# Spreading loads, decay products and routing steps through the attention loop of a three-stage kernel

## The chip, the cores and the metric

One core of one Trainium2 chip runs the whole program. The metric is the device time of one execution in microseconds (us), as the median of several executions. Three executions of the kernel before are given, and one more was profiled.

## The reference

Three layers follow each other, all in fp32, on 3072 tokens (4 batches of 768) of 256 features (8 heads of 32).

```python
def reference(x, a, B, C, ...):
    attn = _attn_ref(x, a, B, C)             # decaying linear attention, per batch and head
    t = attn.transpose(0, 2, 1, 3).reshape(3072, 256)
    t = _moe_ref(t, w_gate, w1, w2)          # 8 experts, each token goes to the best one
    return _moe2_ref(t, probs, v1, v2)       # 4 experts, all of them, mixed by probs

# attention: state (16 x 32) per head;  y_i = C_i . state_i,
#   state_i = a_i * state_(i-1) + outer(B_i, x_i)
# moe:  e = argmax(t @ w_gate);  out = softmax(t @ w_gate)[e] * relu(t @ w1[e]) @ w2[e]
# moe2: out = sum over 4 experts of p_e * relu(t @ v1[e]) @ v2[e]
```

## The kernel before

The program has three stages, one behind the other on TensorE. Stage 1, the attention with the routing of its tokens, takes about the first 105 us of the trace; stage 2, the 8 experts, goes on to about 278 us; stage 3, the 4 dense experts, fills the rest.

**Stage 1** cuts the 3072 tokens into 24 units of 128 (`NU = 24`, six units to a batch, `NCH = 6`), each made of two chunks of 64. The order of its instructions on every engine is the order of the code (`tc.manual_schedule`), and the loop at L728, `for i in range(NU + 2)`, is a software pipeline: iteration i does the last steps of unit i and the first ones of units i+1 and i+2. For a unit u the steps are

- `decay` (L459): TensorE spreads the decays a into `abc`, and a VectorE scan (L465) turns them into `Lt`, the products of decays inside a chunk;
- `decayed_b` (L475): GpSimd multiplies B into `br`, in two halves, one instruction for each chunk;
- `decayed_c` (L549): GpSimd multiplies C, in the padded form `cz`, with the running products `pf` into `Cs`;
- `scores` (L488, L490): TensorE multiplies B and the heads of C (`cm`) into `cb`, and VectorE multiplies with `Lt` into `M`;
- `gain` (L536) and `state` (L544): TensorE sums B x into `U`, and a VectorE scan carries the state `S`, one per chunk;
- `within`, `across`, `copy_y` (L502, L514, L520): TensorE makes `y` from `M` and from `S`, and ScalarE copies it to `yT`;
- `stage_c`, `store` (L560, L568, L569, L570): TensorE transposes `yT` and multiplies it with the gate weights into `tp`, ScalarE takes the logits `lg` and the tokens `xo` out of it, and SyncE's queue stores `xo` to `xs` in DRAM.

The running products `pf` (and `pfg`, the same at the chunk ends) come for three units at a time from `decays_c` (L444, L446, L448): one product `pfp` of TensorE with the selection matrix `sel`. Its other operand is made by `chunk_products` (L388 to L396) once for each half of a batch's length, in tiles named `spare`: a scan in fp32 (L393), its rounding to fp32r by ScalarE (L395), and the rest that the rounding left by GpSimd (L396), so that 64 rows, high parts and rests, enter an fp32r product. The first half is made ahead of the loop, the second in the iterations 0 and 1, and `decays_c(1)` stands in iteration 2 in front of `scores`. All products of this kind share two PSUM buffers named `abc` with `abc` itself and with the counts of the routing.

**Loads** all stand in SyncE's queue: B and x by unit pairs (`load`, L432, L433, 128 and 256 KB), and for three units at once B and C in the transposed form (`load_bc`, L329 to L334: `CT`, `BT`, and C a second time into the two planes of `cz`). The weights of expert 0 come in pieces (`WEIGHTS`, L138); the first weights are split into a high and a low part inside the loop (`split_w`: L154 ScalarE, L160 GpSimd), the second weights behind it (L918 to L920; L154 ScalarE, L158 VectorE). `idd<-zero` (L748) writes 128 words of 4 bytes to DRAM in iteration 8.

**Routing** (`route`) takes the logits of a group of units, finds the expert and the place of each token, and adds the tokens' numbers to the lists `idxf` by small products (`invert`; `om` L226, `ip` L238). `ENDS` names the last units of the groups: 13, 7 and 4 units here, and one more that is empty. The steps of a group are appended to the list `queue`, and `slot` takes one or two of them off at fixed places of each iteration. Behind the first group (`EARLY = 12`) `early` gathers the first 256 tokens of expert 0 from `xs` (`gather`, L280, two indirect DMAs in one step), and eight empty steps later `make_x` transposes them, so that their first product (`ahead`, `pha`) can be made in iteration 24. What is left in `queue` runs behind the loop.

**Stage 2** starts with the 256 early tokens of expert 0 and then needs `idx` (L613), the end of the last group, for the gathers of all others. TensorE does two matmul groups per expert (`ph` L263, `po` L906). **Stage 3** is one dense run of TensorE (L1203, L1264).

These lines set the group ends and the places of the loop's work:

```python
EARLY = 12
ENDS = (12, 19, 23)
    WEIGHTS = {5: (0, 0), 9: (0, 1), 13: (1, 0), 17: (1, 1)}
    SPLITS = {9: 0, 13: 1}
    if i == 2:
        decays_c(1)
    if i % 3 == 1 and has(i + 2) and i > 1:
        decays_c((i + 2) // 3)
    if i == NU:
        ahead(0)
```

Of the kernel before, what the change touches and what calls it, by code (L numbers as in the profile page):

```python
# [8 lines left out]
F32 = mybir.dt.float32  # L9
# [10 lines left out]
P = 128  # L20
# [3 lines left out]
L = 64  # L24
# [9 lines left out]
EARLY = 12  # L34
ENDS = (12, 19, 23)
# [7 lines left out]
def body(tc, I, out):  # L43
    nc = tc.nc
    with ExitStack() as outer:
# [79 lines left out]
        wsp = [outer.enter_context(tc.tile_pool(name="w1s", bufs=1))]  # L125

        def load_w(g, which, j, queue=nc.sync, pieces=1):
# [9 lines left out]
            n = shp[0] // pieces  # L137
            fs = [lambda a=a: queue.dma_start(raw[:, a:a + n], src[:, a:a + n]) for a in range(0, shp[0], n)]  # L138
# [4 lines left out]
        def split_w(g, which, j, parts=1):  # L143
# [158 lines left out]
        with ExitStack() as ctx:  # L302
# [16 lines left out]
            def load_bc(i, cuts=(), queue=nc.sync):  # L319
# [3 lines left out]
                CT = lp.tile([P, HB], F32, tag="CT", name="CT", bufs=3)  # L323
# [4 lines left out]
                def part(a, e, queue=nc.sync):  # L328
                    queue.dma_start(CT[:, a:e], I["CT"][b][:, s0 + a:s0 + e])  # L329
                    queue.dma_start(BT[:, a:e], I["BT"][b][:, s0 + a:s0 + e])  # L330

                def padded(a, e):
                    for m in range(2):
                        nc.sync.dma_start(cz[i % NBC][m::2, m, a:e], I["CT"][b][m::2, s0 + a:s0 + e])  # L334

                def head(h, a, e):
                    nc.scalar.activation(cm[:, h, a:e], CT[:, a:e], AF.Copy, scale=hmask[:, h:h + 1])

                if cuts:
                    return part, padded, head  # L340
                part(0, HB)
                padded(0, HB)
                return [lambda h=h: head(h, 0, HB) for h in range(4)]

            bc_part, bc_padded, bc_head = load_bc(0, (P,))
            bc_part(0, P, nc.scalar)
            d0 = ac.tile([P, 1], F32, name="d0")
# [4 lines left out]
            def spare(tag, dt=F32):  # L352
                return m1.tile([P, 2, 512], dt, tag=tag, name="spare").rearrange("p k c -> p (k c)")[:L, :S]

            a2, d1, pr, prh = spare("xh"), spare("xl").rearrange("p (k i) -> p k i", i=L), spare("xh"), spare("xl", F32R)
            nc.sync.dma_start(a2, I["a2"])
            cz = [ac.tile([P, 2, HB], F32, name=f"cz{k}") for k in range(NBC)]
            NBR = 3
            BW = 2 * P + 2
            brs = [ac.tile([P, 2, BW], F32, name=f"br{k}") for k in range(NBR)]  # L360
            pfg = [ac.tile([P, 3, HD, 3], F32, name=f"pfg{k}") for k in range(3)]
            selF = ac.tile([P, L], F32, name="selF")
            nc.vector.tensor_add(selF, ident[:, :L], ident[:, L:])
            hm8 = ac.tile([P, 4, 2], F32, name="hm8")
            nc.vector.tensor_reduce(hm8, ident.rearrange("p (q n m) -> p q m n", q=4, m=2), axis=AX.X, op=ALU.add)
            hmask = ac.tile([P, 4], F32, name="hmask")
            nc.vector.tensor_add(hmask.rearrange("p (q m) -> p q m", m=2), hm8[:, :2], hm8[:, 2:])
            sel32 = ac.tile([L, L // 2], F32, name="sel32")
            nc.vector.tensor_add(sel32, selF[:L, :L // 2], selF[:L, L // 2:])
            pick = ac.tile([P, 2 * NU, L], F32R, name="pick")  # L370
            delta = ac.tile([P, H, L], F32, name="delta")
            sel = ac.tile([L, NB, P], F32R, name="sel")

            def select(a, e):
                nc.scalar.copy(pick[:, a:e], selF[:, a:e, None].broadcast_to([P, e - a, L]))

            def select_heads(b):
                o = sel[:, b].rearrange("c (q n a) -> c q n a", q=4, a=2)
                nc.scalar.copy(o, sel32[:, b * H:b * H + H].rearrange("c (q a) -> c q a", a=2)[:, :, None, :]
                               .broadcast_to([L, 4, DS, 2]))  # L380

            def chunk_products(h):
# [19 lines left out]
            nc.vector.memset(cz[0], 0.0)  # L402
            select(0, 8)
# [22 lines left out]
            def load(b):  # L426
                bt = lp.tile([P, NCH, P], F32, tag="bt", name="bt")
                x = lp.tile([P, NCH, D], F32, tag="x", name="x")
                x_, b_ = (I[k][b].rearrange("p (c d) -> p c d", c=NCH) for k in ("xt", "bt"))

                def part(a, e):
                    nc.sync.dma_start(bt[:, a:e], b_[:, a:e])  # L432
                    nc.sync.dma_start(x[:, a:e], x_[:, a:e])  # L433

                st[b] = dict(x=x, bt=bt)
                return part
# [3 lines left out]
            def decays_c(i):  # L440
# [3 lines left out]
                nc.tensor.matmul(ps, sel[:, b], prh[:, h * HB:h * HB + HB], start=True, stop=True)  # L444
                PF[i] = lp.tile([P, 3, P], F32, tag="pf", name="pf", bufs=3)
                nc.scalar.copy(PF[i].rearrange("p c i -> p (c i)"), ps)  # L446
                ends = ps.rearrange("p (c k i) -> p c k i", c=3, k=2)[..., L - 1:L].rearrange("p c k o -> p c (k o)")
                nc.scalar.copy(pfg[i % 3][..., 1:], ends[:, :, None, :].broadcast_to([P, 3, HD, 2]))  # L448
# [10 lines left out]
            def decay(u):  # L459

                abc = pa.tile([P, H, L], F32, tag="abc", name="abc", bufs=2)
                nc.tensor.matmul(abc, pick[:, 2 * u:2 * u + 2].rearrange("p c j -> p (c j)"),
# [909 lines left out]
```

## Time and profile before

| what | value |
|---|---|
| three executions | 812.77, 813.72, 806.47 us |
| their median | 812.77 us |
| profiled execution | 806.2 us |
| its span (first to last instruction) | 804.5 us |
| mean granted clock of TensorE | 0.98 |
| PE, DVE, ACT, POOL busy | 95%, 71%, 51%, 59% of the span |

PE is TensorE, DVE VectorE, ACT ScalarE, POOL GpSimd, SP SyncE; SPq rows are the issuing of DMAs from its queue. The span is 1.7 us shorter than the profiled execution's time. The three executions lie at two levels, and the profiled one lies at the lower. TensorE's clock has two levels, 1.2 and 2.4 GHz; a granted clock of 1.00 is the higher one all through a stretch, 0.50 the lower one.

### The profile page before, as it was taken

To read this page: it belongs to the slowest core of one execution; us is meant where nothing else is said; L and a number is where in the kernel's file an instruction comes from. 1 tells how busy PE (TensorE), PEld (TensorE's weight loads), DVE (VectorE), ACT (ScalarE), POOL (GpSimd) and SP (SyncE) were. 2 spreads that over 40 slices of the span, in tenths; PEclk is the share of its full clock that TensorE was granted. 3 is DMA by queue.
4 is the path that set the end of the run, shared out by engine and by line. 5 is a ranking of instruction groups with operands and counts; after the bars stand their busy time and mean duration, and the time that the engine had idled before them with its cause. 6 is when DMAs were issued, how large, how long until landed. Compare 5 with 4: busy or idle time off the path is not lost.

```text
span 804.5 us, 17552 instructions
## 1 busy us (share of the span) xinstructions
PE 767.7 (95%) x6891; PEld 722.8 (90%) x6891; DVE 567.5 (71%) x983; ACT 411.4 (51%) x903; POOL 472.0 (59%) x533
## 2 busy tenths in 40 slices
PE   7989878999999999999999999999999999999994
PEld 5555568889999889999999999999999999999994
DVE  7646763784456678678796777887777977778853
ACT  4755343444455465546655455556455555554540
POOL 6546625835776065448866366786355877475634
PEclk9989988999999999999999999999999999999997
DMA  6584324546533300000101000000000100000001
GB/s 191 155 177 142 95 31 157 191 124 96 156 119 95 91 27 27 2 1 27 32 23 27 1 1 27 28 27 27 1 1 1 53 2 2 1 34 21 27 27 53
DMA packets 42117, 46.62 MB, mean 58 GB/s; under 512 B 10928, under 2 KB 30512, under 8 KB 42032
## 3 DMA queue, kind: packets, MB, share of 16 engines
q1 hardware_dynamic: 37328, 37.16, 17.2%
q0 software_dynamic: 3360, 7.13, 2.9%
q10 hardware_dynamic: 1344, 1.18, 0.5%
q8 instruction: 55, 0.90, 0.5%
q14 instruction: 30, 0.25, 0.1%
HBM read 39.10 MB, written 6.35 MB: 56 GB/s over the span
## 4 chain that ended last, share of the span: by engine, by line
PE 62%; ACT 1%; DVE 1%; issue 0%; POOL 0%; POOLq 0%; DVEq 0%; ACTq 0%
PE po L1264 33%; PE x L1203 9%; PE z L1203 8%; PE w L1203 8%; PE y L1203 4%; PE poA L1264 0%; ACT s L1216 0%; ACT xc L849 0%; POOLq L1368 0%; ACT h L1209 0%; DVE h L1212 0%; DVE ts L840 0%; DVE c L1230 0%; DVE c L1238 0%; POOL out L1284 0%
## 5 line engine op out<-in xcount | busy, mean ns | idle before, releaser
L1264 PE MATMUL po<-w,h 128*128 128x256 f32 x2280 | 280.0, 280 | 0.3 <-DVE h L1212 0.3
L1264 PEld LDWEIGHTS po<-w,h 128*128 128x128 f32 x2280 | 277.5, 188 | 0.5 <-DVE h L1212 0.5
L1209 ACT ACTIVATE h<-c 128x384 fp32r<-128x384 f32 x192 | 98.8, 525 | 150.2 <-DVE c L1238 85.0
L1212 DVE SCALAR_TENSOR_TENSOR h<-c,h 128x384 fp32r<-128x384 f32 x192 | 149.6, 788 | 11.5
L1221 POOL TENSOR_TENSOR g<-s,s 128x384 f32<-128x384 f32 x64 | 65.1, 1017 | 150.5 <-ACT s L1220 148.7
L1223 DVE TENSOR_TENSOR u<-y,s 128x384 f32<-128x384 f32 x64 | 35.5, 555 | 70.0 <-ACT s L1220 65.1
L1203 PE MATMUL x<-xc,wh 128*128 128x384 f32 x256 | 67.0, 342 | 3.6 <-ACT s L1216 1.5
L1203 PE MATMUL w<-xc,wh 128*128 128x384 f32 x256 | 66.0, 338 | 0.5 <-ACT xc L849 0.4
L1203 PE MATMUL z<-xc,wh 128*128 128x384 f32 x256 | 65.4, 337 | 0.0
L160 POOL TENSOR_TENSOR wl<-raw,wh 128x1024 fp32r<-128x1024 f32 (+1 forms) x22 | 39.6, 1801 | 40.7 <-ACT wh L154 29.0
L850 POOL TENSOR_TENSOR xc<-x,xc 128x384 fp32r<-128x384 f32 x32 | 36.9, 1153 | 44.5 <-ACT xc L849 44.2
L885 ACT ACTIVATE hh<-ph 128x216 fp32r<-128x216 f32 (+8 forms) x68 | 33.5, 494 | 51.2 <-PE ph L263 43.4
L1238 DVE TENSOR_TENSOR c<-u,g 128x384 f32<-128x384 f32 x64 | 59.3, 927 | 0.0
L1216 ACT COPY s<-x 128x384 f32<-128x384 f32 x64 | 30.6, 478 | 52.3 <-PE x L1203 51.9
L887 DVE SCALAR_TENSOR_TENSOR hl<-ph,hh 128x216 fp32r<-128x216 f32 (+8 forms) x68 | 37.6, 558 | 24.3 <-ACT hh L885 24.2
L1212 DVE SCALAR_TENSOR_TENSOR h<-x,h 128x384 fp32r<-128x384 f32 x64 | 35.7, 558 | 24.5 <-ACT h L1209 24.2
L850 POOL TENSOR_TENSOR xc<-ts,xc 128x384 fp32r<-128x384 f32 x46 | 52.3, 1149 | 0.0
L263 PE MATMUL ph<-xh,wh 128*128 128x488 f32 (+8 forms) x142 | 49.4, 351 | 1.1 <-ACT xo L569 0.6
L263 PE MATMUL ph<-xl,wh 128*128 128x488 f32 (+8 forms) x142 | 49.5, 348 | 0.0
L263 PE MATMUL ph<-xh,wl 128*128 128x488 f32 (+8 forms) x142 | 49.2, 347 | 0.0
L1203 PEld LDWEIGHTS x<-xc,wh 128*128 128x128 f32 x256 | 42.2, 188 | 7.7 <-ACT s L1216 5.3
L906 PE MATMUL po<-hh,wh 128*128 128x488 f32 (+8 forms) x142 | 48.8, 343 | 0.0
(245 smaller groups left out, 1704.9 us busy)
## 6 DMA issues: line engine op xcount, KB each, us to landing
raw<-in_w SPq DMA_DIRECT2D x26, 512.0 KB, 4.0
raw<-in_v SPq DMA_DIRECT2D x32, 256.0 KB, 2.7
x<-in_xt SPq DMA_DIRECT2D x12, 256.0 KB, 3.3
xs<-xo SPq DMA_DIRECT2D x24, 128.0 KB, 2.5
bt<-in_bt SPq DMA_DIRECT2D x12, 128.0 KB, 2.3
CT<-in_CT SPq DMA_DIRECT2D x7, 192.0 KB, 3.0
BT<-in_BT SPq DMA_DIRECT2D x7, 192.0 KB, 2.9
cz<-in_CT SPq DMA_DIRECT2D x14, 96.0 KB, 4.0
```

Of the source, the lines that this page charges most:

```text
L160: ins = nc.gpsimd.tensor_sub(lo[:, :, a:a + n], raw[:, :, a:a + n], hi[:, :, a:a + n].bitcast(F32))
L263: mm = nc.tensor.matmul(ph, w[:, k, fs], x[k], start=(i == 0), stop=(i == 5))
L850: eng.tensor_sub(o[:, 1], src, o[:, 0].bitcast(F32))
L887: i1 = nc.vector.scalar_tensor_tensor(hl, ph, 0.0, hh.bitcast(F32), op0=ALU.max, op1=ALU.subtract)
L906: mm = nc.tensor.matmul(po, w[:, f % 4, ks], h, start=(i == 0), stop=(i == 23))
L1203: nc.tensor.matmul(bank[to], w[:, a], x[:, r], start=(m == 0 and to not in seen), stop=(m == 2), skip_group_check=True)
L1209: sc.activation(HP[n][0], src, AF.Relu)
L1212: v.scalar_tensor_tensor(HP[n][1], src, 0.0, HP[n][0].bitcast(F32), op0=ALU.max, op1=ALU.subtract)
L1221: nc.gpsimd.tensor_add(g_, s5, s7)
L1223: v.tensor_add(u2, bank["y"], s1)
L1238: v.tensor_add(c22, u2, g_)
L1264: nc.tensor.matmul(two[h], x[:, ts], w2[:, w, j], start=(i, j, h * (len(hs) - 1), m) == (0, 0, 0, 0), stop=(i, j, m) == (3, 1, 2), skip_gr ...
```

## The change

What it does, part by part:

- **Loads.** B and x come by single units, four units ahead (64 and 128 KB). `CT` is gone: the heads of C are made from `cz`. Of `BT` and the two planes of `cz` one is issued per iteration. The weights of expert 0 come as sixteen pieces of 128 KB, one per iteration from iteration 3 to 18; of the first weights a piece is now a quarter of the columns.
- **Decays.** `chunk_products` ends with the scan; `pfp` is one fp32 product of 32 rows. L395 and L396 are gone. The seven `decays_c` of the loop stand in the iterations 2, 3, 4, 5, 6, 9 and 12, behind `decay`; ahead of the loop the order of the first units is changed. `pick` (eleven casts ahead) becomes `pk`, one small cast per unit.
- **Routing.** The groups are 12, 7 and 5 units. The counting of `early` moves into the first group's steps, and `ie`, the two gathers and `make_x` are taken one per iteration. `ahead(0)` is called behind the loop.
- **Expert 0's second weights** are split inside the loop, in eight pieces, ScalarE the high and GpSimd the low parts.

The diff, cut to its core:

```diff
-EARLY = 12
-ENDS = (12, 19, 23)
+EARLY = 11
+ENDS = (11, 18, 23)
...
+            n, c = shp[0], shp[1] // pieces
+            if which:
+                n, c = shp[0] // pieces, shp[1]
...
-                if which:
+                if which and parts == 1:
                     nc.vector.tensor_sub(lo[:, :, a:a + n], raw[:, :, a:a + n], hi[:, :, a:a + n].bitcast(F32))
                     return
...
-                CT = lp.tile([P, HB], F32, tag="CT", name="CT", bufs=3)
...
-                    nc.scalar.activation(cm[:, h, a:e], CT[:, a:e], AF.Copy, scale=hmask[:, h:h + 1])
+                    nc.scalar.activation(cm[:, h, a:e], cz[i % NBC][:, h % 2, a:e], AF.Copy, scale=hmask[:, h // 2:h // 2 + 1])
...
                 def products():
                     nc.vector.tensor_tensor_scan(pr[:, s], a2[:, s], d1[:, k].rearrange("p k i -> p (k i)"), 0.0,
                                                  op0=ALU.mult, op1=ALU.add)
-                    nc.scalar.copy(prh[:, s], pr[:, s])
-                    nc.gpsimd.tensor_sub(prh[L // 2:, s], pr[L // 2:, s], prh[L // 2:, s].bitcast(F32))
...
+            def load(u):
+                b, c = divmod(u, NCH)
...
+                nc.sync.dma_start(st[b]["bt"][:, c], I["bt"][b].rearrange("p (c d) -> p c d", c=NCH)[:, c])
+                nc.sync.dma_start(st[b]["x"][:, c], I["xt"][b].rearrange("p (c d) -> p c d", c=NCH)[:, c])
...
-                nc.tensor.matmul(ps, sel[:, b], prh[:, h * HB:h * HB + HB], start=True, stop=True)
+                nc.tensor.matmul(ps, sel[:, b], pr[:, h * HB:h * HB + HB], start=True, stop=True)
...
-                ] + invert(rt, sl, g0, n, NC, finish, psum, rest=2 if last else 5)
+                ] + list(between) + invert(rt, sl, g0, n, NC, finish, psum, rest=2 if last else 3)
...
+                return ([count, None, shift],
+                        [lambda: nc.vector.tensor_scalar(ie, idxf[:, 0:2], float((EARLY + 1) * P - 1), None, op0=ALU.min)]
+                        + [lambda k=k: gather(0, (k,), xs[:(EARLY + 1) * P], ie) for k in range(2)] + [None]
+                        + [lambda: make_x(0, (0, 1), psum_a)])
...
+            for h in range(4):
+                bc_head(h, P, HB)
+            warm(2)
             decay(1)
-            warm(4)
             decays_c(0)
...
+            WEIGHTS = {3: (0, 0), 7: (0, 1), 11: (1, 0), 15: (1, 1)}
+            SPLITS = {8: (0, 0), 12: (0, 1), 16: (1, 0), 20: (1, 1)}
+            DECAYS = {max(m + 1, 3 * m - 9): m for m in range(1, NU // 3)}
...
+                if has(i + 4):
+                    load(i + 4)
...
                 if has(i + 2):
                     decay(i + 2)
+                if i < 2:
+                    chunks[2 + i]()
+                if i in DECAYS:
+                    decays_c(DECAYS[i])
+                if has(i + 1):
+                    decayed_c(i + 1)
+                for f in gathers[:1]:
+                    if f:
+                        f()
+                gathers = gathers[1:]
                 slot(2)
...
-                if i == NU:
-                    ahead(0)
...
+                    between, after = early() if i - 2 == EARLY else ((), ())
+                    queue += route(*GROUPS[i - 2], psum_a, between)
+                    if after:
+                        queue.append(lambda after=after: gathers.extend(after))
+            assert not gathers
+            ahead(0)
             queue += route(*GROUPS[NU - 1], psum_p)
...
-            for j in range(2):
-                for f in split_w(0, 1, j):
-                    f()
```

Three places of the order on the engines follow. On TensorE, at the end of iteration 1 and in iteration 2 (`pfp` is the product of the running decays for the units 3 to 5, `cb` the scores of unit 3), before:

```order
L514 MATMUL y<-Cs,S 32x128 x8
L536 MATMUL U<-x,br_145 32x32 x16
L560 MATMUL tp<-rhsT_179,yT 128x136
L560 MATMUL tp<-rhsT_180,yT 128x136
L444 MATMUL pfp<-spare,sel 128x384
L488 MATMUL cb<-cm,BT 64x256 x4
L462 MATMUL abc<-ah,pick 128x512
```

and now:

```order
L507 MATMUL y<-Cs,S 32x128 x8
L529 MATMUL U<-x,br_146 32x32 x16
L553 MATMUL tp<-rhsT_184,yT 128x136
L553 MATMUL tp<-rhsT_185,yT 128x136
L481 MATMUL cb<-cm,BT 64x256 x4
L455 MATMUL abc<-ah,pk 128x512
L437 MATMUL pfp<-spare,sel 128x384
```

`pfp` has moved behind the scores and the `abc` of the same iteration.

On GpSimd, about the two gathers of expert 0's early tokens (`wl` is a low part of its weights, `ex` a routing step), before:

```order
L475 TENSOR_TENSOR br_145<-bt,Lt 64x2x64 x2
L549 TENSOR_TENSOR Cs<-cz_140,pf 128x256
L475 TENSOR_TENSOR br_143<-bt,Lt 64x2x64 x2
L549 TENSOR_TENSOR Cs<-cz_141,pf 128x256
L280 DMA xg<-xs,ie 128x256 x2
L475 TENSOR_TENSOR br_144<-bt,Lt 64x2x64 x2
L549 TENSOR_TENSOR Cs<-cz_141,pf 128x256
```

and now:

```order
L163 TENSOR_TENSOR wl_0_1_1978<-raw_0_1_1537,wh_0_1_1977 128x4x64
L468 TENSOR_TENSOR br_146<-bt,Lt 64x2x64 x2
L542 TENSOR_TENSOR Cs<-cz_130,pf 128x256
L283 DMA xg<-xs,ie 128x256
L610 TENSOR_TENSOR ex<-lg,mx 128x56
L163 TENSOR_TENSOR wl_0_1_1978<-raw_0_1_1537,wh_0_1_1977 128x4x64
L468 TENSOR_TENSOR br_147<-bt,Lt 64x2x64 x2
L542 TENSOR_TENSOR Cs<-cz_130,pf 128x256
L283 DMA xg<-xs,ie 128x256
```

The two gathers stand in two units, and every unit there has a `wl` as well.

On VectorE, at the start of the second group's routing (`mx` is its first step; 128x7 is the group of seven units, 128x4 the last of four), before:

```order
L490 TENSOR_TENSOR M<-cb,Lt 128x512
L544 SCALAR_TENSOR_TENSOR S<-pfg_147,U 128x96
L158 TENSOR_TENSOR wl_0_0_2329<-raw_0_0_1317,wh_0_0_2328 128x1024
L297 TENSOR_TENSOR xl<-tpx,xh 128x2x256
L623 TENSOR_REDUCE mx<-lg 128x7
L624 TENSOR_TENSOR eq<-lg,mx 128x56
L158 TENSOR_TENSOR wl_0_1_2333<-raw_0_1_1675,wh_0_1_2332 128x1024
L625 TENSOR_TENSOR eq<-eq,rev 128x56
L623 TENSOR_REDUCE mx<-lg 128x4
```

and now:

```order
L537 SCALAR_TENSOR_TENSOR S<-pfg_151,U 128x96
L616 TENSOR_REDUCE mx<-lg 128x7
L483 TENSOR_TENSOR M<-cb,Lt 128x512
L617 TENSOR_TENSOR eq<-lg,mx 128x56
L458 SCALAR_TENSOR_TENSOR Lt<-abc,delta 128x512
L618 TENSOR_TENSOR eq<-eq,rev 128x56
L619 TENSOR_REDUCE m_2051<-eq 128x7
L620 TENSOR_TENSOR oneh<-eq,m_2051 128x56
L621 TENSOR_REDUCE red<-oneh 128x8
L537 SCALAR_TENSOR_TENSOR S<-pfg_151,U 128x96
```

The second group's first steps have moved from behind the last unit to between the units 21 to 23; the two `wl` of VectorE are gone.

## Rows read from the trace of the kernel before

**Rows 1.** The page: the span, and the chain that ended last by line.

```profile
span 804.5 us, 17552 instructions
...
PE po L1264 33%; PE x L1203 9%; PE z L1203 8%; PE w L1203 8%; PE y L1203 4%; PE poA L1264 0%; ACT s L1216 0%; ACT xc L849 0%; POOLq L1368 0%; ACT h L1209 0%; DVE h L1212 0%; DVE ts L840 0%; DVE c L1230 0%; DVE c L1238 0%; POOL out L1284 0%
```

**Rows 2.** Timeline, ScalarE's copies yT of units 0, 1, 8, 23: start, duration.

```profile
15.47 0.37 ACT L520 COPY yT<-y 128x256 f32<-128x256 f32 x1 [0.81 <-PE y L514]
21.66 0.35 ACT L520 COPY yT<-y 128x256 f32<-128x256 f32 x1
...
44.07 0.37 ACT L520 COPY yT<-y 128x256 f32<-128x256 f32 x1 [1.07 <-PE y L514]
...
104.63 0.37 ACT L520 COPY yT<-y 128x256 f32<-128x256 f32 x1
```

**Rows 3.** Timeline of the start: start, duration, in brackets the wait before it.

```profile
9.25 0.99 POOL L396 TENSOR_TENSOR spare<-spare 32x384 fp32r<-32x384 f32 x1 [1.82 <-DMA bt<-in_bt]
...
13.26 0.66 PE L488 MATMUL cb<-cm,BT 64*64 64x256 f32 x8 [1.11 <-ACT cm L337]
...
20.56 0.99 POOL L396 TENSOR_TENSOR spare<-spare 32x384 fp32r<-32x384 f32 x1 [2.79 <-ACT spare L395]
...
21.60 0.43 PE L444 MATMUL pfp<-spare,sel 64*128 64x384 f32 x1 [1.75 <-POOL spare L396]
```

**Rows 4.** Windows: length, busy PE PEld DVE ACT POOL, granted clock, DMA share, GB/s.

```profile
47.00:54.00 7.00, 4.96 (x130) 3.25 (x126) 2.68 (x4) 2.49 (x9) 2.24 (x4) 1.00 0.89 62
54.00:62.00 8.00, 7.29 (x120) 4.25 (x111) 2.83 (x5) 3.83 (x13) 3.99 (x8) 0.59 0.77 237
...
104.00:109.00 5.00, 3.30 (x25) 2.65 (x22) 3.86 (x10) 3.92 (x11) 1.22 (x3) 1.00 0.21 59
109.00:118.00 9.00, 6.44 (x61) 5.98 (x61) 7.71 (x30) 3.02 (x10) 4.43 (x11) 0.94 0.29 21
...
124.00:130.00 6.00, 3.67 (x20) 2.95 (x19) 1.88 (x7) 0.58 (x1) 4.55 (x5) 0.76 0.39 109
```

**Rows 5.** Timeline of the stall in units 10 and 11.

```profile
44.85 0.58 SPq L748 DMA_DIRECT2D idd<-zero  x1
...
50.52 0.35 DVE L544 TENSOR_TENSOR_SCAN S<-pfg,U 128x96 f32<-128x96 f32 x1 [2.96 <-PE pfp L444]
...
53.78 0.38 PE L536 MATMUL U<-x,br 128*32 128x32 f32 x15 [1.69 <-issue]
```

**Rows 6.** Instructions by line and form, 0 to 125 us: busy, mean ns, idle before.

```profile
L475 POOL TENSOR_TENSOR br<-bt,Lt 64x128 f32<-64x128 f32 x48 | 20.7, 431 | 14.4 <-DVE Lt L465 8.1 <-PE abc L462 2.6 <-DMA xg<-xs,ie 1.8
L560 PE MATMUL tp<-rhsT,yT 128*128 128x136 f32 x96 | 18.5, 318 | 0.0
L549 POOL TENSOR_TENSOR Cs<-cz,pf 128x256 f32<-128x256 f32 x24 | 18.0, 750 | 2.1 <-POOL br L475 0.4
...
L160 POOL TENSOR_TENSOR wl<-raw,wh 128x256 fp32r<-128x256 f32 x8 | 5.8, 730 | 15.5 <-ACT lg L568 9.6 <-ACT wh L154 3.9 <-ACT yT L520 1.9
...
L444 PE MATMUL pfp<-spare,sel 64*128 64x384 f32 x8 | 3.5, 437 | 3.0 <-POOL spare L396 1.7 <-DVE Lt L465 1.3
```

**Rows 7.** Timeline, 85 to 99 us: VectorE's routing and the gathers.

```profile
85.05 1.72 POOL L475 TENSOR_TENSOR br<-bt,Lt 64x128 f32<-64x128 f32 x2 [1.67 <-DVE Lt L465]
...
87.73 0.66 PE L514 MATMUL y<-Cs,S 32*32 32x128 f32 x16 [1.19 <-DVE S L544]
...
92.93 1.21 POOL L280 DMA_INDIRECT xg<-xs,ie  x1 [0.76 <-DVE S L544]
...
98.12 0.33 PE L536 MATMUL U<-x,br 128*32 128x32 f32 x16 [1.90 <-POOL br L475]
```

**Rows 8.** Timeline behind the loop, 107 to 122 us.

```profile
107.30 1.23 DVE L158 TENSOR_TENSOR wl<-raw,wh 128x1024 fp32r<-128x1024 f32 x1 [0.35 <-DMA xs<-xo]
...
108.12 0.41 ACT L569 COPY xo<-tp 128x264 f32<-128x264 f32 x1
...
121.83 0.17 DVE L613 CAST idx<-idxf 128x5 int32<-128x5 f32 x1
```

More of the change, by code (lines that the diff above doesn't have):

```diff
@@ L136, in load_w @@
             RAW[g, which, j] = raw
-            n = shp[0] // pieces
-            fs = [lambda a=a: queue.dma_start(raw[:, a:a + n], src[:, a:a + n]) for a in range(0, shp[0], n)]
+            n, c = shp[0], shp[1] // pieces
+            if which:
+                n, c = shp[0] // pieces, shp[1]
+            fs = [lambda a=a, o=o: queue.dma_start(raw[:, a:a + n, o:o + c], src[:, a:a + n, o:o + c])
+                  for a in range(0, shp[0], n) for o in range(0, shp[1], c)]
             if pieces > 1:
@@ L366, in body @@
[L366 to L370, printed above, removed]
+            hm4 = ac.tile([P, 4], F32, name="hm4")
+            nc.vector.tensor_reduce(hm4, ident.rearrange("p (q n) -> p q n", q=4), axis=AX.X, op=ALU.add)
@@ L401, in body @@
                 nc.gpsimd.memset(t, 0.0)
-            nc.vector.memset(cz[0], 0.0)
-            select(0, 8)
+            nc.vector.memset(cz[0][:, :, P:], 0.0)
+            for u in range(3):
+                select(u)
             nc.scalar.copy(delta, selF[:, None, :].broadcast_to([P, H, L]))
@@ L570, in store, with route @@
                 nc.sync.dma_start(xs[u * P:u * P + P].rearrange("t (k d) -> t k d", k=2), xo[:, :, :P])
-            def route(g0, n, psum):
+            def route(g0, n, psum, between=(), after=()):
                 v, g = nc.vector, nc.gpsimd
@@ L704, in body @@
             warm(7)
-            for f in chunk_products(0):
+            chunks = chunk_products(0) + chunk_products(1)
+            for f in chunks[:2]:
                 f()
@@ L722, in body @@
                 nc.gpsimd.tensor_copy(rhsT[k][:, (0, E1)[k]:(P, E1 + P)[k]], ident)
-            pend, later, products_1 = {}, [], chunk_products(1)
-            WEIGHTS = {5: (0, 0), 9: (0, 1), 13: (1, 0), 17: (1, 1)}
-            SPLITS = {9: 0, 13: 1}
-            ws = []
+            heads = {0: [lambda h=h: bc_next[0][2](h) for h in range(2)],
+                     1: [lambda h=h: bc_next[0][2](h) for h in range(2, 4)]}
+            stage, fetch = {}, []
+            for m in range(2, NU // 3):
+                stage[max(3 * m - 7, 0)] = m
+            ws, gathers = [], []
+            WEIGHTS = {3: (0, 0), 7: (0, 1), 11: (1, 0), 15: (1, 1)}
+            SPLITS = {8: (0, 0), 12: (0, 1), 16: (1, 0), 20: (1, 1)}
+            DECAYS = {max(m + 1, 3 * m - 9): m for m in range(1, NU // 3)}
+            bcs = []
             for i in range(NU + 2):
@@ L730, in body @@
                     store(i - 2)
-                b = i // NCH + 1
-                if 0 < b < NB and i % NCH == 1:
-                    part = load(b)
-                if 0 < b < NB and i % 2 == 1:
-                    part(i % NCH - 1, i % NCH + 1)
-                m = 2 if i == 0 else (i + 7) // 3 if i % 3 == 2 else 0
-                if 2 <= m < NU // 3:
-                    pend[max(3 * m - 5, 1)] = load_bc(m)
-                bg = bg + pend.pop(i, [])
+                if has(i + 4):
+                    load(i + 4)
+                if i in stage:
+                    bc = load_bc(stage[i])
+                    bcs = bcs + [bc[0]] + [lambda m=m, bc=bc: bc[1](m) for m in range(2)]
+                    for k in range(2):
+                        heads[3 * stage[i] - 3 + k] = [lambda h=h, bc=bc: bc[2](h) for h in range(2 * k, 2 * k + 2)]
+                for f in bcs[:1]:
+                    f()
+                bcs = bcs[1:]
                 if i in WEIGHTS:
-                    later += load_w(0, *WEIGHTS[i], pieces=2 + 2 * WEIGHTS[i][0])
-                for f in later[:1]:
-                    f()
-                later = later[1:]
-                if i == 3:
+                    fetch += load_w(0, *WEIGHTS[i], pieces=4)
+                for f in fetch[:1]:
+                    f()
+                fetch = fetch[1:]
+                if i == 2:
                     nc.sync.dma_start(dpr, I["dp"].rearrange("p (u e) -> p u e", u=NU))
```

136 lines of the change are left out of this document (58 added, 78 removed).

## The prediction

> **What bounds the kernel now.** The first view is the page with its chain of waits: TensorE ends the program, and a third of the span is one line of stage 3 [rows 1]. The change touches nothing there, nor in stage 2 behind its first expert, so the question is what it does to the first 138 us. The second view is the timeline of one instruction that comes once per unit, ScalarE's copy `yT` [rows 2]. Its first start, 15.47, is the length of the start. From unit 1 (21.66) to unit 8 (44.07) there are seven intervals, 22.41 us, so 3.20 us a unit where little disturbs. From unit 1 to unit 23 (104.63) there are 22 intervals, 82.97 us; at 3.20 they would take 70.4. So the loop holds 12.6 us of disturbance, and the interval from unit 0 to unit 1, 6.19 us, holds another 3.0.
>
> The timeline tells where. In the start, `cb` of unit 1 waits 1.11 us for ScalarE's heads `cm`, and the second half of the running products keeps TensorE waiting 1.75 us for GpSimd's subtraction, which itself waited for ScalarE's rounding [rows 3]. In the units 10 and 11 the state scan waits 2.96 us and `U` stops for 1.69 us in the middle with nothing named [rows 5]; the DMA engines are then 89% busy while they move 62 GB/s, and TensorE runs afterwards at a granted clock of 0.59 for 8 us, after the window in which it was busy 4.96 us of 7.00 [rows 4]. The waits are 4.65 us, the clock costs at most 0.41 x 8 = 3.3; I count 6.4 for both. `pfp` waited 1.3 us in the loop for a PSUM buffer that `Lt` held [rows 6]. VectorE's routing steps delay a state scan so that `y` waits 1.19 us, and the gathers on GpSimd delay `br` so that `U` waits 1.90 us [rows 7]. This is 10.8 of the 12.6 us.
>
> Behind the loop the third view, busy time by windows, shows TensorE idle for 1.70, 2.56 and 2.33 us in the three stretches 104 to 109, 109 to 118 and 124 to 130, together 6.6 us, with a granted clock of 0.76 in the last [rows 4]. What it waits for is the routing: the tokens of unit 23 are copied at 108.12, and the last indices come at 121.83 [rows 8].
>
> **The change part by part. Start.** The rounding and the subtraction (0.99 us, two times [rows 3]) are gone from both halves, and the four heads of unit 1 stand ahead of the copies of `pf`. In unit 0 `cb` of unit 1 then starts when the heads have landed in ScalarE's queue: I take 2.0 us off 15.47, between 0 (the heads now hang on the padded loads of C, which a DMA wait like the 1.82 us before the subtraction could make late) and 2.1 (0.99 + 1.11). In unit 1 the wait of 1.75 us goes, and `pfp` moves behind the scores; of the 2.99 us over the normal interval I take 2.5, between 1.75 and 2.99. Late next is VectorE, whose scan stands there still. Start: -4.5, bounds -5.1 and -1.75.
>
> **Decays in the loop.** Seven products `pfp` change from fp32r to fp32. The row of before has 437 ns [rows 6]; the nearest fp32 row is `tp`, 18.5 us for 48 products of 136 columns (two records each), 0.385 us each, so 1.09 for 384 columns. The added cost lies between 0 and 0.65 us each; `tp` has the type in question, so I stay near it with 0.5: 7 x 0.5 = +3.5, bounds 0 and +4.6. It lies on TensorE, which nothing hides. Behind `abc` of the same iteration `pfp` takes a buffer whose reader is an iteration old: the 1.3 us go. The casts `pk` replace those of `pick` on ScalarE, which is busy 3.83 us of 8 in a loop window [rows 4]; I cost them at nothing, as I do the heads out of `cz`.
>
> **Routing in the loop.** Each gather has its own unit. GpSimd then does two `br`, `Cs`, a `wl` and a gather: 0.86 + 0.75 + 0.73 + 1.21 = 3.55 us [rows 6, 7] against 3.20, so 0.35 in each of two units, +0.7 for the 1.90 us that go: -1.2. Queued behind a gather are the `wl`, and `br` of the next unit, for which `U` waits. If each of the two waits as the one before, it is 3.8 for 1.9: bounds -1.9 and +1.9. The second group's first steps, some nine small ones of VectorE, now stand between scans and scores of the units 21 to 23, +0.5 (0 to +2). The `om` steps and their 1.19 us stay.
>
> **Second weights.** The `wl` of VectorE behind the loop (1.23 us, two times [rows 8]) go, and eight of GpSimd come (0.73 each [rows 6]), one a unit. Without a gather the unit has 2.34 us of GpSimd's work under 3.20, so TensorE covers it; without that cover it is 0.73 each.
>
> What such a `wl` does to VectorE can be weighed. Two `br` beside the routing's `om` took 1.72 us [rows 7], against 2 x 0.431 [rows 6]: 0.86 lost in one meeting. The Trainium skill, "SBUF — State Buffer", section "SBUF: two separate sides", has for it that an operation of VectorE with two SBUF inputs and one of GpSimd that reads SBUF lock the same port pair for a whole instruction, and the other blocks. The trace agrees. By the rule eight new `wl` could cost 8 x 0.73 = 5.8 us if each met such an operation on the path; by the rows only the units with `om` have them, and `Lt` and `M` read PSUM, so the sum holds nothing for it.
>
> **Loads.** The bytes fall (`CT` is gone), the pieces get smaller and even. SyncE's queue has to issue five in an iteration with a weight piece; at the 0.58 us of the one issue shown [rows 5] that is 2.9, under 3.20, so it costs nothing as long as an issue stays under 0.64. The stall of units 10 and 11 begins a little behind the write of 128 words `idd<-zero` [rows 5], which stays in iteration 8; I let the whole 6.4 us stay, bounds 0 and -6.4.
>
> Loop: +3.5 - 1.3 - 1.2 + 0.5 = +1.5, bounds -9.6 (all 6.4 go, `pfp` free, gathers free) and +7.2.
>
> **Behind the loop.** With `ahead(0)` behind it, `tp` of unit 23 no longer waits for the early products, nor ScalarE for the two big halves; its copy at 108.12 comes 3.49 us behind `yT`. I take 1.7 off. The last indices come 13.7 us later [rows 8]; half of the second group's steps are then done, and both `wl` of 1.23 us are gone, so some 8.5 should do: -5. TensorE has its own work there, though, and idles only 6.6 us in all [rows 4], so of the 6.7 us I count 5. The granted clock of 0.76 in the 6 us behind 124 costs up to 0.24 x 6 = 1.4 there; without the waits I count 1 of it. Behind the loop: -6, bounds -8 and -2.
>
> **Sum.** -4.5 + 1.5 - 6 = -9.0 us, from the profiled execution's 806.2 (its span 804.5 and 1.7 around it) to 797.2. The median of the executions before, 812.77, lies 6.6 us over the profiled one, since two of three are at an upper level. From the median it would be 803.8. Which level the new median takes I can't tell from one profile; I forecast 800, between the two.
>
> **The rivals.** *The stall goes too.* For it: it stands in the stretch with the most loads of a kind, and they become even. Against it: 62 GB/s at 89% busy looks like many tiny packets, which stay. If it goes, it is 6.4 less: 794.
>
> *The loop gives it back.* `pfp` costs 4.6 instead of 3.5, both gathers wait 1.9 us (+3.1 against my sum), and TensorE's own work or new waits hold the end of stage 1 to half (+3). That is 7.2 of the 9.0: 807, not to be told from no change. For it: GpSimd's 3.55 us is over a unit's 3.20, and the page has TensorE busy for most of what I want to save.
>
> *The feed becomes the bound.* From iteration 3 to 18 a unit's transfers are B 64, x 128, a weight piece 128, a third of `BT` and `cz` (128 on average) and the store 128 KB, 576 KB. In 3.20 us that is 184 GB/s. The trace has 237 GB/s in one window and 62 in the one before it [rows 4], a mean of 155. At 157 GB/s a unit takes 3.76 us and sixteen of them eat the 9.0 us; below that it is slower than before. At 130 it is 4.54 us, 16 x 1.34 = 21.4 more: 821. Against it: before, units of nearly these bytes ran at 3.20 us, loads lead by four units, and the weak window was 7 us short. The Trainium skill speaks for it in "DMA: Bandwidth & Descriptors", section "Measured (HBM→SBUF, 128 partitions, SWDGE, issued from GpSimd)": transfers should be gathered into large ones, and small ones are ruled by their descriptors; it gives 138 GB/s for 64 KB. By that figure a unit would take an estimated 4.27 us, and the kernel would be slower. The trace's 237 GB/s, with pieces of 128 to 256 KB and several under way, says that single transfers add up; no run here shows it for 64 KB.
>
> **How the numbers follow.** The forecast has 0.45, the stall that goes 0.20, the loop that gives it back 0.25, the feed 0.10. What a measurement of this kernel can tell from no change is about 1%, so faster means under 804.6 and slower over 820.9. Nearly all of the first case, the second and a little of the third are faster: 0.66. The third and the forecast's edge are the same: 0.25. The feed is slower: 0.09. The range goes from 787 (the stall goes, the median is at the lower level) to 812 (the third case at the upper level).
>
> **What would show it.** Right: `yT` of unit 0 near 13.5 and of unit 1 near 17; 22 intervals of 83 to 85 us in all; the state scan still waiting in the units 10 and 11; `pfp` near 0.9 us; the last indices some 9 us behind the last copy `xo`; TensorE idle for under 2 us between the loop and the first gathered tokens. Wrong: intervals of over 4 us all through the iterations 3 to 18, with `x`, `bt` or `raw` named as what is waited for (the feed); `U` waiting for `br` in the units 21 to 23 (GpSimd); `y` waiting for the state behind routing steps (VectorE).

## The result and the profile after

The kernel after takes 802.84 us (median of 20 executions, 796.37 to 809.59), the kernel before 812.37 us (20 executions, 804.45 to 818.09). The ratio is 0.9899, with a 95% interval from 0.9872 to 0.9927: about 8 us faster by the ratio, 9.5 by the medians. The forecast was 800 us, in a range from 787 to 812, with 9.0 us of gain by its sum.

The two profiled executions tell about half of it. The one of after took 801.08 us with a span of 799.4, so the spans differ by 5.1 us only. The profiled execution of before lies 6.2 us under the median of its kernel, that of after 1.8 us under. A second profile of after (the run `a_same` below) has a span of 800.9. Of 35 executions of before that were timed beside the first experiments, the faster half takes 808.8 us on average at a mean granted clock of 0.979, the slower half 814.6 us at 0.973. So stages are compared here over several profiles, and sizes by ratios.

The first view is the timeline of ScalarE's copies `yT` after (start and duration), the units 0, 1, 8 and 23, as in [rows 2]:

```profile
16.44 0.37 ACT L513 COPY yT<-y 128x256 f32<-128x256 f32 x1 [1.12 <-PE y L507]
19.26 0.37 ACT L513 COPY yT<-y 128x256 f32<-128x256 f32 x1
...
44.55 0.37 ACT L513 COPY yT<-y 128x256 f32<-128x256 f32 x1 [1.25 <-PE y L507]
...
103.13 0.37 ACT L513 COPY yT<-y 128x256 f32<-128x256 f32 x1 [1.26 <-PE y L507]
```

Unit 1 is 2.4 us earlier than before (21.66), unit 8 half a microsecond later, unit 23 1.5 us earlier. The interval from unit 0 to unit 1 went from 6.19 to 2.82 us. The first start, 16.44, is later than before. That belongs to this one execution: in the nine other profiles of after and of kernels made from it that keep the fp32 product it lies between 13.1 and 15.3. Its `cb` of unit 0 took 1.13 us, against 0.66 in `a_same`; the granted clock reads 1.00 in both from 8 to 13 us, so why it took longer is open. On the timeline:

```profile
8.65 1.13 PE L481 MATMUL cb<-cm,BT 64*64 64x256 f32 x8
...
11.00 0.91 PE L437 MATMUL pfp<-spare,sel 32*128 32x384 f32 x2
```

The same copies in the second profile of after, from `a_same`, the units 0, 1 and 23:

```profile
13.29 0.37 ACT L513 COPY yT<-y 128x256 f32<-128x256 f32 x1 [0.25 <-PE y L507]
16.96 0.34 ACT L513 COPY yT<-y 128x256 f32<-128x256 f32 x1
...
103.21 0.37 ACT L513 COPY yT<-y 128x256 f32<-128x256 f32 x1 [1.27 <-PE y L507]
```

There unit 1 starts 4.7 us earlier than before, and the 22 intervals that follow take 86.25 us against 82.97.

The windows of after, with the columns of [rows 4]:

```profile
47.00:54.00 7.00, 6.57 (x188) 4.02 (x186) 4.17 (x6) 5.54 (x19) 4.58 (x9) 1.00 0.50 74
54.00:62.00 8.00, 5.79 (x96) 2.85 (x95) 3.56 (x5) 1.24 (x5) 3.02 (x6) 0.77 0.60 152
104.00:109.00 5.00, 2.29 (x24) 1.95 (x25) 3.34 (x14) 1.36 (x5) 2.23 (x6) 1.00 0.20 58
109.00:118.00 9.00, 8.44 (x67) 8.24 (x66) 5.77 (x21) 4.23 (x13) 5.41 (x8) 0.81 0.32 22
124.00:130.00 6.00, 3.81 (x32) 3.45 (x31) 1.34 (x4) 1.99 (x5) 0.59 (x1) 1.00 0.73 218
```

The weak stretch of the units 10 and 11 is still there, some microseconds later: 5.79 busy of 8 us. Behind the loop TensorE idles for 2.71, 0.56 and 2.19 us, 5.5 in all against 6.6. The last stretch has its full clock now (1.00 against 0.76), but the one from 109 to 118 us has less (0.81 against 0.94).

The last copy of tokens and the last indices, as in [rows 8], from the timeline:

```profile
105.53 0.40 ACT L562 COPY xo<-tp 128x264 f32<-128x264 f32 x1
...
113.76 0.47 DVE L606 CAST idx<-idxf 128x5 int32<-128x5 f32 x1
```

They stand 8.2 us apart; before it was 13.7. Stage 3 begins at 273.4 us against 278.3.

### The profile page after: what moved, and what is told of

Read it like the earlier page. It is cut to its first block, busy times and chain, and to the rows that moved or that the text cites. A ratio compares the mean times of both kernels' runs of the same rounds, so it can differ in the third digit from the quotient of the medians.

```text
span 799.4 us, 17665 instructions
## 1 busy us (share of the span) xinstructions
PE 769.5 (96%) x6895; PEld 721.6 (90%) x6895; DVE 561.5 (70%) x981; ACT 413.6 (52%) x920; POOL 474.9 (59%) x539
## 4 chain that ended last, share of the span: by engine, by line
PE 60%; ACT 1%; POOL 1%; issue 1%; DVE 1%; POOLq 0%; DVEq 0%; ACTq 0%
PE po L1268 32%; PE x L1207 9%; PE z L1207 8%; PE w L1207 8%; PE y L1207 4%; POOL out L1288 1%; ACT s L1220 0%; DVE h L1216 0%; ACT xc L856 0%; ACT h L1213 0%; PE poA L1268 0%; DVE c L1234 0%; POOLq L1372 0%; DVE c L1242 0%; DVE xc L857 0%
## 5 line engine op out<-in xcount | busy, mean ns | idle before, releaser
L163 POOL TENSOR_TENSOR wl<-raw,wh 128x256 fp32r<-128x256 f32 (+1 forms) x30 | 45.6, 1518 | 41.6 <-ACT wh L157 40.6
```

## The experiments

Twelve runs were made in three groups, each beside runs of the kernel before on the same chip. The edits below are against the kernel after, or against the kernel before where the name begins with `b`. All ratios are to the kernel before.

**Second weights back behind the loop (`a_late_w2`).**

```diff
-            SPLITS = {8: (0, 0), 12: (0, 1), 16: (1, 0), 20: (1, 1)}
+            SPLITS = {8: (0, 0), 12: (0, 1)}
...
+            for j in range(2):
+                for f in split_w(0, 1, j):
+                    f()
```

> The kernel after, with the split of expert 0's second weights put back behind the loop (ScalarE two halves, VectorE two halves). Theory 1 (the gain behind the loop comes from the routing groups, the second weights are a side matter): the two VectorE halves of 1.2 us delay the routing chain by up to 2.4 us, of which TensorE's own work covers about half, and GpSimd is relieved by 0.73 us in eight units: +1 us against the kernel after, a ratio to the kernel before of 0.991. Rival (the second weights are what pays): the last indices come at 118 instead of 113.8 us and the kernel is 4 us or more slower than after, a ratio of 0.995.

Measured: 0.9915 (0.9883 to 0.9947), 804.83 us. The first theory's value; the difference to after is within the intervals. The last indices came at 112.2 us in its profile, not at 118, and 8.2 us behind the last token copy as in after, so the rival is out.

**The old groups (`a_groups`).**

```diff
-EARLY = 11
-ENDS = (11, 18, 23)
+EARLY = 12
+ENDS = (12, 19, 23)
```

> The kernel after, with the routing groups of 13, 7 and 4 units of before. Theory 1: the second group's routing falls behind the loop again, the last indices come 4 to 8 us later behind the last token copy than in the kernel after (8.2 us), TensorE waits for the gathered tokens again and its clock falls there: +3 to +5 us, a ratio of 0.994 to 0.996. Rival (TensorE's own work bounds the stretch behind the loop): +0 to +1 us, 0.990 to 0.991.

Measured: 0.9922 (0.9888 to 0.9956), 804.05 us. The mechanism shows in its profile: `idx` comes at 117.7 us, 13.0 us behind the last token copy, and stage 3 begins at 279.8. But that profiled execution, 806.94 us, is 2.9 us over the median, and by the ratio the size lies between the two theories and is not clear of after.

**High and low parts of the decays again (`a_hilo`).**

```diff
+                    nc.scalar.copy(prh[:, s], pr[:, s])
+                    nc.gpsimd.tensor_sub(prh[L // 2:, s], pr[L // 2:, s], prh[L // 2:, s].bitcast(F32))
...
-                nc.tensor.matmul(ps, sel[:, b], pr[:, h * HB:h * HB + HB], start=True, stop=True)
+                nc.tensor.matmul(ps, sel[:, b], prh[:, h * HB:h * HB + HB], start=True, stop=True)
```

> The kernel after, with the running products of decays in 64 rows of fp32r again (rounding by ScalarE, subtraction by GpSimd), pfp at 0.44 us instead of 1.0. Theory 1: seven products in the loop get 0.56 us shorter on TensorE, 3.9 us; the rounding and the subtraction come back in the start, where unit 0 pays about 1.2 us, and in iteration 1, where pfp now stands behind the scores and hides them: 2 to 3 us faster than after, a ratio of 0.987. Rival (the one fp32 product is part of the gain): 1 to 3 us slower than after, 0.992.

Measured: 0.9958 (0.9921 to 0.9996), 808.51 us: slower than after, where I expected it faster. The interval just overlaps that of after, and the median is 3.7 to 4.9 us over those of the three other kernels of its group (`a_late_w2`, `a_groups`, `a_pairs`). The timeline of this kernel, in iteration 1:

```profile
19.41 0.51 ACT L395 CAST spare<-spare 64x384 fp32r<-64x384 f32 x1 [2.72 <-DVE spare L393]
...
21.25 0.35 ACT L517 COPY yT<-y 128x256 f32<-128x256 f32 x1
21.40 0.66 PE L485 MATMUL cb<-cm,BT 64*64 64x256 f32 x8 [2.31 <-ACT cm L337]
```

The rounding waits 2.72 us in ScalarE's queue for VectorE's scan. Behind it in that queue stand the heads `cm` and the copy `yT` of unit 1, so TensorE's scores wait 2.31 us for the heads, although the product `pfp` itself had been moved out of the way. Unit 1 starts at 21.25 instead of 16.96 us (`a_same`), 4.3 us late. Of these, 1.8 us stand already in unit 0 (15.07 against 13.29), and 2.5 us come in the interval from unit 0 to unit 1, where this wait lies. By unit 9 the shorter products have given 1.5 us back (27.99 us from unit 1 to unit 9 against 29.53), by unit 23 nothing of that is left (86.44 against 86.25). What the change removed in iteration 1 was an instruction that waits at the head of a queue, not only a link of the chain to `pfp`.

**The same alone on the kernel before (`b_decay`).**

```diff
-                    nc.scalar.copy(prh[:, s], pr[:, s])
-                    nc.gpsimd.tensor_sub(prh[L // 2:, s], pr[L // 2:, s], prh[L // 2:, s].bitcast(F32))
...
-                nc.tensor.matmul(ps, sel[:, b], prh[:, h * HB:h * HB + HB], start=True, stop=True)
+                nc.tensor.matmul(ps, sel[:, b], pr[:, h * HB:h * HB + HB], start=True, stop=True)
```

> The kernel before, with the running products of decays in one fp32 product of 32 rows and nothing else changed. Theory 1 (the rounding in ScalarE's queue holds up the heads of C and with them the scores, in unit 0 and once more in unit 1): the interval from unit 0 to unit 1 falls from 6.2 to 3 to 4 us and the start by 1 us, against 7 x 0.56 = 3.9 us of longer products: within 2 us of before, 0.998 to 1.001, as the rest of the change is needed to move the products off the first units' path. Rival (the decays alone carry the gain): 0.994.

Measured: 0.9991 (0.9962 to 1.0019), 806.94 us. By the size it is the first theory: the interval from unit 0 to unit 1 is 3.29 us in its profile, and the loop behind it is 4.3 us longer than before (87.30 us from unit 1 to unit 23 against 82.97). The 1 us at the start did not come: `yT` of unit 0 starts at 16.88, against 15.47 in the profile of before. The price of a product is plain in the table of instructions of after, eight products of two records each, to be held against [rows 6]:

```profile
L437 PE MATMUL pfp<-spare,sel 32*128 32x384 f32 x16 | 8.0, 582 | 0.0
```

8.0 us by 8 is 1.0 us against 0.437, so 0.56 more each; nothing waits for a buffer any more.

**Loads by pairs (`a_pairs`).**

```diff
-                if has(i + 4):
-                    load(i + 4)
+                if has(i + 4) and i % 2 == 0:
+                    load(i + 4, 2)
...
-                    fetch += load_w(0, *WEIGHTS[i], pieces=4)
+                    fetch += load_w(0, *WEIGHTS[i], pieces=2)
```

> The kernel after, with B and x loaded for two units at once (128 and 256 KB, every second iteration) and the weights of expert 0 in eight pieces of 256 KB instead of sixteen of 128 KB, so as uneven as before; C is still loaded once. Theory 1 (the loads are hidden either way): within 1 us of after, 0.989 to 0.991. Rival (the even loads are what pays): 3 us or more slower than after, 0.994 and more, with waits for x, bt or weights in the loop.

Measured: 0.9906 (0.9873 to 0.9939), 803.63 us. The spread of the loads is worth nothing that these runs can tell, either way.

**Both gathers in one step (`a_gath`, and again as `a_gath2`).**

```diff
-                        + [lambda k=k: gather(0, (k,), xs[:(EARLY + 1) * P], ie) for k in range(2)] + [None]
+                        + [lambda: gather(0, (0, 1), xs[:(EARLY + 1) * P], ie)] + [None] * 2
```

> The kernel after, with both early gathers in one step of iteration 21. Theory 1: GpSimd holds br of the next unit for 1.2 us more in that unit, U waits 1 to 2 us as in the kernel before and the next iteration is relieved: +1 us, 0.991. Rival (the separate gathers are a main part of the gain): +3 us, 0.994.

> Both early gathers in one step again, now beside after on the same chip, since the first comparison left 1 to 5 us open. Theory 1: +1 us against after, of which U waits 2 us for br once. Rival (the separate gathers are a main part of the gain): +3 us or more.

Measured: 0.9961 (0.9921 to 1.0002) in the first group, 0.9889 (0.9841 to 0.9938) in the second, where after itself had 0.9897. The two do not agree well. The comparison beside after shows no gain from separate gathers, and the first leaves up to 5 us. The profiles tell what `U` waits for `br` at that place: 2.8 us before, 0.8 after and 1.0 in `a_same`, and with both gathers in one step 2.2 in `a_gath` and 1.0 in `a_gath2`. So at most some 1.4 us of the difference stand in this wait, and not in every execution; the rest stays unsettled, with the second as the better comparison.

**The write of 128 words as one row (`a_idd`, `b_idd`).** The long intervals of the units 10 to 12 stood in every profile of both kernels. In after the queue and TensorE looked like this (SPq rows are issues of DMAs):

```profile
47.58 0.45 SPq L753 DMA_DIRECT2D idd<-zero  x1
...
49.38 3.23 SPq L429 DMA_DIRECT2D x<-in_xt  x1
...
57.14 0.51 PE L507 MATMUL y<-Cs,S 32*32 32x128 f32 x9 [2.21 <-issue]
```

The DMA view of after, 46 to 60 us in 40 equal slices, has the busy share of the DMA engines in tenths, and what they moved:

```profile
DMA  3650634839831000002119900001769389999731
GB/s 101 190 161 23 197 103 135 210 45 149 239 98 38 0 0 0 0 21 31 22 47 99 6 0 0 0 0 20 116 161 146 95 277 345 326 309 252 239 107 40
```

In 14 of the 16 slices from 50.2 to 55.8 us the engines are busy for at most two tenths. In before they were 89% busy in the weak window [rows 4].

```diff
-                    nc.sync.dma_start(idd[NT:], zero)
+                    nc.sync.dma_start(idd[NT:NT + P - 1].rearrange("p o -> o p"), ident[P - 1:, :P - 1].bitcast(I32))
+                    nc.sync.dma_start(idd[NT + P - 1:], zero[:1])
```

> The kernel after, with the 128 words written to DRAM in iteration 8 as one row of 127 words and one word instead of 128 single words. In all five profiles so far the units 10 to 12 take 6 to 7 us more than their share, and the DMA engines move 0 to 60 GB/s there, soon behind this write. Theory 1 (the write of single words clogs the DMA engines, and what TensorE waits for there with nothing named is held up behind it): the long intervals of the units 10 to 12 fall to 3.0 to 3.5 us, the kernel gets 5 us faster than after, a ratio to the kernel before of 0.984. Rival (something else of that stretch, the number of transfers or a fixed place of the program): the long intervals stay, 0.990.

> The kernel before, with the same one edit of the 128 words. Theory 1 (the write of single words): the long intervals of the units 10 to 12 go here too, 5 us faster, a ratio of 0.994. Rival (something else in that stretch): 1.000 and the intervals stay.

Measured: before with this edit 0.9943 (0.9905 to 0.9981), 801.06 us; after with it 0.9887 (0.9835 to 0.9938), 799.05 us. On the kernel before the size and the intervals are those of the first theory. What is shown by this is that the write causes the stall; that it clogs the DMA engines is not, since in after they stood mostly idle. Its copies `yT` of the units 9 to 12, on the timeline:

```profile
48.04 0.37 ACT L520 COPY yT<-y 128x256 f32<-128x256 f32 x1 [1.14 <-PE y L514]
51.61 0.37 ACT L520 COPY yT<-y 128x256 f32<-128x256 f32 x1
54.49 0.37 ACT L520 COPY yT<-y 128x256 f32<-128x256 f32 x1 [0.72 <-PE y L514]
57.34 0.37 ACT L520 COPY yT<-y 128x256 f32<-128x256 f32 x1 [1.22 <-PE y L514]
```

Three intervals of 3.57, 2.88 and 2.85 us stand where before had 6.78, 4.92 and 4.33, 6.7 us less, and TensorE's clock in the stretch 45 to 66 us is 1.00 against 0.84 (windows, columns as in [rows 4], first with the edit, then the kernel before):

```profile
45.00:66.00 21.00, 21.00 (x617) 13.35 (x615) 14.40 (x23) 14.21 (x49) 13.96 (x26) 1.00 0.74 212
```

```profile
45.00:66.00 21.00, 18.25 (x412) 10.94 (x415) 9.89 (x15) 8.78 (x31) 9.51 (x18) 0.84 0.67 134
```

On the kernel after the 0.984 of the theory did not come, and the ratio is not told from that of after: another stall came out in unit 12, 7.82 us long. ScalarE's timeline of `a_idd` names it:

```profile
59.98 0.61 ACT L337 ACTIVATE cm<-cz,hmask 128x384 f32<-128x384 f32 x1 [2.95 <-DMA cz<-in_CT]
```

**The order of the loads of C (`a_order`, `a_best`, `a_same`).** The second plane of `cz` is issued one iteration ahead of the heads that read it. After waits there too, in unit 18, where the interval is 6.54 us (4.84 in `a_order`, where nothing waits):

```profile
84.12 0.67 SPq L334 DMA_DIRECT2D cz<-in_CT  x1
...
87.30 0.62 ACT L337 ACTIVATE cm<-cz,hmask 128x384 f32<-128x384 f32 x1 [1.59 <-DMA cz<-in_CT]
```

```diff
-                    bcs = bcs + [bc[0]] + [lambda m=m, bc=bc: bc[1](m) for m in range(2)]
+                    bcs = bcs + [lambda m=m, bc=bc: bc[1](m) for m in range(2)] + [bc[0]]
```

`a_order` has this edit, `a_best` this and the one of `a_idd`, `a_same` none.

> The kernel after once more, unchanged, beside the next three on the same chip. Theory (the start is shortened by what was forecast, and the one profile of after caught a half-clock stretch there): yT of unit 1 starts at 17 to 18 us instead of 19.3, the units 10 to 12 are long again, the ratio is 0.990. Rival (the start of after is as slow as its first profile showed): yT of unit 1 at 19 us or later.

> The kernel after, with the two planes of cz loaded ahead of BT in each group of three units instead of behind it, nothing else. In four of the six kernels built on after, ScalarE's heads waited 0.6 to 2.9 us for cz, which is issued one iteration ahead; in none of the three built on before. Theory 1 (making the heads from cz took a lead of several iterations away, and the loop pays for it): no wait of the heads for a DMA is left and the kernel is 1 to 2 us faster than after, 0.988. Rival (the waits are hidden behind others): the same as after, 0.990.

> The kernel after with both edits: cz ahead of BT, and the 128 words as one row of 127 and one word. Theory 1 (both stalls are real and separate, and the one came out when the other went): units 10 to 13 all between 2 and 4.9 us, 6 us faster than after, a ratio of 0.982. Rival (a stall in that stretch comes back in another guise whatever is taken out): 0.988 to 0.990.

Measured: `a_same` 0.9897 (0.9858 to 0.9936), 804.64 us; `a_order` 0.9875 (0.983 to 0.992), 800.75 us; `a_best` 0.9844 (0.9798 to 0.989), 799.43 us. In the profiles of `a_order` and `a_best` no head waits for a DMA in the loop. The gain of `a_order` alone has the expected size but is not clear of after. `a_best` has the lowest ratio of all, and its median is 5.2 us under that of `a_same` in the same group; the two intervals overlap, and 0.9844 lies between the theory's 0.982 and the rival's 0.988. Its copies of the units 9 to 13:

```profile
46.37 0.37 ACT L513 COPY yT<-y 128x256 f32<-128x256 f32 x1
48.61 0.38 ACT L513 COPY yT<-y 128x256 f32<-128x256 f32 x1
51.81 0.37 ACT L513 COPY yT<-y 128x256 f32<-128x256 f32 x1 [1.25 <-PE y L507]
56.55 0.37 ACT L513 COPY yT<-y 128x256 f32<-128x256 f32 x1
58.80 0.39 ACT L513 COPY yT<-y 128x256 f32<-128x256 f32 x1
```

Both stalls are gone, which speaks against the rival: four intervals of 12.4 us together, where the two profiles of after have 19.3 (after, 49.34 to 68.68) and 20.3 (`a_same`). Not all of it reaches the end: unit 23 comes 7.0 us earlier than in `a_same`, stage 3 only 4.6 us.

## Why the prediction was right, and where it was not

**The sum.** A gain of 9.0 us was forecast and 9.5 is measured by the medians, 8 by the ratio. The step that halved the distance between the two levels was not needed: 803.8, the sum taken from the median, is nearer to 802.84 than the 800 on record. One profile and three times were too few to speak of two levels; the 20 executions of before are spread from 804 to 818.

That the sizes agree so well is in part luck. The terms were worked out on a profile, and on the profiles they come to less. In the first profile of after they are -2.4 us (start, to unit 1), +0.9 (loop, to unit 23), -3.4 (from there to stage 3) and -0.2 (the rest), together -5.1; in `a_same` -4.7, +3.3, -2.7 and +0.5, together -3.6. What is missing to 9.5 lies in how far each profiled execution stands under its median. The lower end of the range, 787, is also further down than the terms give: 797.2 less 6.4 is 790.8.

**Start (-4.5).** Right. Unit 1 starts at 16.8 to 17.9 us in eight of the ten profiles of after and of kernels made from it that keep the fp32 product, 3.7 to 4.8 us earlier than in the profile of before (21.66; `b_idd`, which has the same start, has 22.40). The first profile of after (19.26) and that of `a_gath2` (18.94) are later. The cause was only partly right. I priced the rounding and the subtraction as links ahead of `pfp`; `a_hilo` shows that with `pfp` out of the way the rounding still costs the unit, because it waits at the head of ScalarE's queue and the heads of C stand behind it. That is why my expectation for `a_hilo` failed.

**Decays in the loop (+3.5).** The price of a product is right: 0.56 us each for seven is 3.9, and the wait for a PSUM buffer went. That all of it reaches the length of the loop is shown on the kernel before only: there `b_decay` has the loop 4.3 us longer. In `a_hilo`, with the short products, the loop is no shorter than in `a_same`.

**Loop (+1.5).** The sum is near in the first profile of after, 83.87 against 82.97 us, +0.9, and too small in the second, +3.3. In all seven profiles of after and of kernels made from it that keep the fp32 product, the write of 128 words and the order of the loads of C, it is +0.9 to +3.7. The gathers came as forecast or better: `U` waits 0.8 us for `br` there; before it waited 2.8 us in that unit, of which I had counted 1.90. For the eight `wl` of the second weights, which I cost at nothing, `a_late_w2` shows no cost that it can tell. The stall of units 10 to 12 stayed, as the forecast let it. What I did not see is the new wait: I cost the heads out of `cz` at nothing and named only ScalarE's free time as their cover. In the profile of before `CT` was issued 6.2 to 9.2 us ahead of its first head in the loop; the second plane of `cz` now has one iteration of lead (84.12 to 87.30 us, 3.2, in unit 18), and the heads waited 1.59 us in after and up to 2.95 in its variants. In none of the three profiles of before and of kernels made from it did they wait for a load in the loop.

**Behind the loop (-6).** The indices came earlier as forecast, but the time that this gives was mis-sized. The last indices stand 8.2 us behind the last token copy, where 8.5 was forecast. But from `yT` of unit 23 to the start of stage 3 it is 170.3 us against 173.7, 3.4 us less, and 171.1 in `a_same`. Over all profiles it is less still: the nine with after's code behind the loop have 169.9 to 175.2 us, median 171.2, and the three with before's 171.9 to 173.7, median 172.7. TensorE still idles 5.5 us in the three stretches where I had counted 5 of the 6.6 us as gone. Between the loop and the first gathered tokens it waits 3.5 us, not under 2 as I wrote: 2.0 us of it for VectorE's `om`, before the early products. Later it waits twice, 3.2 us in all, for the low parts `hl`. Waits of TensorE, 103 to 140 us (engine and line waited for, sum, times, longest), after:

```profile
PE ph L266 <- DVE hl L894: 3.2, 2, 1.7
PE ip L241 <- DVE om L229: 2.3, 2, 2.0
```

and before:

```profile
PE ip L238 <- DVE om L226: 2.6, 1, 2.6
PE tpx L293 <- DMA xg<-xs,idx: 1.9, 2, 1.4
```

So the wait for `om` stayed, that for the gathered tokens went, and the one for `hl` came. `a_groups` has the groups' own share at 0.9922 against 0.9899, some 2 us, not clear of zero.

**The rivals.** The stall did not go by itself; it went when its cause, the write, was changed. The feed did not become the bound: no intervals of over 4 us all through the iterations 3 to 18, no wait for `x`, `bt` or `raw` in the loop, and `a_pairs` is not told from after. The loop gave back 0.9 to 3.7 us, short of the 5.7 of the rival, and in another place than I named. But the rival's last part came: TensorE's waits held the gain behind the loop to 3.4 and 2.7 us, about half of the 6.

**What stays open.** The two profiles differ by 5.1 us and the medians by 9.5. Where the rest lies no profile here shows, nor whether the granted clock that falls with the longer times is its cause. Five parts were undone one by one, and only `a_hilo` stands apart from after, by its median; what second weights, groups and gathers are worth singly lies below what these runs resolve.

## What to carry to other kernels

An instruction that waits at the head of an in-order queue costs everything behind it, so ask of a removed step not only who reads its result but who stands behind it. When one copy of an input takes over the readers of two, carry over the lead of the earlier load as well: put the load that has the earliest reader first. A stall that stays at one place through every variant deserves its own experiment; here one line outside the change was worth, by the ratio on the kernel before, half as much as the whole change.

## What the runs showed of the hardware that was not expected

One DMA that writes 128 single words of 4 bytes, 512 bytes in all, was followed in after by several microseconds in which the DMA engines moved mostly 0 to 50 GB/s and a later issue in the same queue took 3.23 us (with the row the longest issue between 45 and 66 us took 2.3 us in `b_idd`, 2.0 in `a_idd`). Written as one row and one word, the same data brought the kernel before to 0.9943 (0.9905 to 0.9981) of its time. TensorE stopped in such stretches in the middle of runs of like products with nothing named as what it waited for. Between 40 and 105 us all eleven profiles with the single words have such a stop of over 1 us, the longest of each 1.3 to 2.9 us; the three with the row (`b_idd`, `a_idd`, `a_best`) have none over 0.7. Why the stops go with the slow transfers was not tried.
